# Reordering the front part of an attention kernel: which engine normalizes, which maxima come first, and how many are done when the loop begins

## The chip, the cores and the metric

The kernel runs on one core of a Trainium2 chip. The metric is the device time of one launch in microseconds (us), median over several runs. The engines are TensorE (PE, with PEld for its weight loads), VectorE (DVE), ScalarE (ACT), GpSimd (POOL) and SyncE (SP), which here issues nearly all transfers. Each engine takes its instructions strictly in the order in which the program lists them.

## The reference

One transformer layer on `x` of 2048 rows by 512 columns, in float32. It has 32 heads of 16 dimensions that share one key and one value head.

```
mod = silu(c) @ w_mod                      # six vectors: sa, ca, ga, sb, cb, gb
h = layernorm(x) * (1 + ca) + sa
q = h @ wq;  k = h @ wk;  v = h @ wv
o = softmax(q k^T / 4) v                   # for each of 32 heads
x = x + ga * (o @ wo)
h = layernorm(x) * (1 + cb) + sb
x = x + gb * (gelu(h @ w1 + b1) @ w2 + b2)
```

## The kernel before, in words

**Precision.** Products of full precision are made of three products of rounded operands: a tile is split into a high part (rounded) and a low part (the remainder), and high x high, low x high and high x low are added in one bank (`mm3`, line 162). A "set" below is such a group of three.

**Units and the loop.** The attention is cut into 64 units: eight blocks of 256 query rows, and in each block eight groups of four heads. The order of work is written out by hand: the program is recorded in the order in which Python issues it, and each engine keeps that order. A unit needs first the maximum of each row of scores, found by *max products*: a matmul of queries and 512 keys into one of three PSUM buffers named m (line 505), and a reduction on DVE (line 510). There are 32 for each unit, half of them on the upper 64 rows of the PE array and half on the lower 64, where pairs run side by side. When a unit's 32 are done, `put_max` reduces them once more (558), transposes (559), arranges the result (`gather`, 553), splits it into a high part mh and a low part ml, and sends these as extra rows into the unit's query tile `qst` (548): the score product of the exponentials (line 607) then comes out with the maximum subtracted, and ACT takes the exponentials (611). Products with the values (628) add to the unit's output.

The loop goes over units, in pairs of steps, four pairs for each unit. A pair holds eight score products and eight exponentials for its unit, and some max products for later units; beside these it holds pieces of query projections (line 191), whose result DVE copies out (456). How far the max products run ahead is set by `lead`: `lead[0]` is 32 + 4 x `LEAD_0` (56 done when the loop begins), and for the first eight units it rises evenly to 312 at the ninth; in a pair, the number issued is rounded to an even number.

**The front part.** Before the loop, x is loaded in four blocks of 512 rows, and for each block b:

- `stats1`: mean and variance on DVE (199 to 205), inverse root on POOL (207), and the factors for ACT (354, 355);
- `xhat1`: the normalized rows, four row tiles, on DVE, ACT (364) or POOL (366);
- `heads`: for each quarter of the columns, transposes (`turn1`, 373), modulation on ACT (`mod1`, 379), rounding (132 on ACT or 130 on POOL) and remainder (137);
- `keys`: four sets against the joined key and value weights (162), then `kv_out`: two casts of the keys into `ks` (394) and a copy to `vt` (395), both on ACT;
- `low_k`: the low part of the keys on DVE, written to rows 32 to 48 of `ks` (400); `repeat_k`: ACT copies it to rows 96 to 112 (404), for the lower half of the array;
- `v_out`: transposes of the values (412) and a copy (413).

Once block b's keys stand in `ks`, max products with 512 more keys can be made. So the front runs max products of the first two units between the other steps. `FIRST_MAX` gives their order as pairs of unit and block of keys; `SLOTS` gives the order of everything else: each entry is a number of max products, and then the named steps. "q 1" is a query projection, "rows" the late modulation rows (290), "wq" a weight's preparation. `keep_warm` issues filler matmuls (285). At the end of the front come the first score products (607, at 74.85 us in the trace).

## Time and profile before

| what | value |
|---|---|
| median of 3 runs | 1565.62 us (1565.11 to 1568.13) |
| span of the profiled execution, first to last instruction | 1563.1 us |
| the profiled execution's own time | not listed apart from its span |
| granted TensorE clock, mean | 1.000 |
| PE busy | 1546.5 us (99%) |
| DVE busy | 1401.7 us (90%) |
| ACT busy | 1228.8 us (79%) |
| POOL busy | 681.7 us (44%) |
| first score product of the loop | 74.85 us |

The times in the trace count from the span's start. A busy share is an average over stages: the front part (to about 75 us), the loop over 64 units, and the end. A row of the timeline gives the start, the length, the engine, the line of the kernel, the operation, the tile written and the tiles read, and how many instructions were merged into the row (x4); in brackets stands the idle time before it, and who ended it.

### The profile page before, as it was taken

To read this page: it belongs to the slowest core of one execution; us is meant where nothing else is said; L and a number is where in the kernel's file an instruction comes from. 1 tells how busy PE (TensorE), PEld (TensorE's weight loads), DVE (VectorE), ACT (ScalarE), POOL (GpSimd) and SP (SyncE) were. 2 spreads that over 40 slices of the span, in tenths; PEclk is the share of its full clock that TensorE was granted. 3 is DMA by queue.
4 is the path that set the end of the run, shared out by engine and by line. 5 is a ranking of instruction groups with operands and counts; after the bars stand their busy time and mean duration, and the time that the engine had idled before them with its cause. 6 is when DMAs were issued, how large, how long until landed. Compare 5 with 4: busy or idle time off the path is not lost.

```text
span 1563.1 us, 41433 instructions
## 1 busy us (share of the span) xinstructions
PE 1546.5 (99%) x16387; PEld 959.9 (61%) x16387; DVE 1401.7 (90%) x2479; ACT 1228.8 (79%) x2392; POOL 681.7 (44%) x1194
## 2 busy tenths in 40 slices
PE   7999999999999999999999999999999999999999
PEld 4455555567655665557655675556655676556667
DVE  7999999999999999999999999999999999999625
ACT  5577778788777887788877887788877888788853
POOL 5545433877323570246422472245611573235711
PEclk9999999999999999999999999999999999999999
DMA  7235412313030211213022120303112130312241
GB/s 244 97 96 194 152 52 89 120 52 97 19 110 19 83 60 35 93 29 99 29 62 69 57 84 26 105 16 97 43 50 79 46 97 20 102 34 66 81 150 61
DMA packets 83126, 121.63 MB, mean 78 GB/s; under 512 B 19614, under 2 KB 56222, under 8 KB 82676
## 3 DMA queue, kind: packets, MB, share of 16 engines
q1 hardware_dynamic: 82916, 118.97, 23.5%
q8 instruction: 130, 2.13, 0.6%
q14 instruction: 64, 0.52, 0.1%
q10 hardware_dynamic: 16, 0.00, 0.0%
HBM read 91.13 MB, written 27.27 MB: 76 GB/s over the span
## 4 chain that ended last, share of the span: by engine, by line
PE 84%; DVE 10%; issue 3%; POOL 2%; DMA 1%; ACT 0%; ACTq 0%; SPq 0%; POOLq 0%; DVEq 0%
PE acc L628 28%; PE m L505 24%; PE e L607 16%; DVE mx L510 8%; PE w1ps L191 8%; PE w2ps L181 2%; PE w2ps L191 1%; PE w1ps L181 1%; DMA xt<-in_A_x_dram 1%; PE qps L191 1%; PE tp L191 1%; PE wops L191 1%; PE kps L162 1%; DVE st L835 1%; DVE x L828 1%
## 5 line engine op out<-in xcount | busy, mean ns | idle before, releaser
L510 DVE TENSOR_REDUCE mx<-m 128x1 f32<-128x512 f32 x2048 | 1270.5, 682 | 86.9 <-PE m L505 63.8
L611 ACT ACTIVATE p<-e 128x512 f32<-128x512 f32 x2048 | 1099.3, 598 | 257.4 <-PE e L607 110.5
L505 PE MATMUL m<-ks,qst 64*128 64x512 f32 x2048 | 832.4, 429 | 1.9 <-DVE mx L510 0.6
L607 PE MATMUL e<-qst,ks 64*128 64x512 f32 x2048 | 747.6, 412 | 0.1
L628 PE MATMUL acc<-p,va 128*32 128x256 f32 x8192 | 548.0, 385 | 0.0
L505 PEld LDWEIGHTS m<-ks,qst 64*128 64x128 f32 x2048 | 366.5, 184 | 212.3 <-DVE mx L510 174.8
L607 PEld LDWEIGHTS e<-qst,ks 64*128 64x128 f32 x2048 | 362.5, 184 | 95.2 <-ACT p L611 71.1
L628 PEld LDWEIGHTS acc<-p,va 128*32 128x32 f32 x8192 | 213.7, 109 | 213.1 <-issue 110.0
L553 POOL TENSOR_SCALAR mt<-turned 8x32 f32<-8x32 f32 x256 | 53.1, 208 | 418.9 <-DVE turned L559 406.9
L191 PE MATMUL w1ps<-h2H,w1t 64*128 64x256 f32 x1232 | 235.6, 287 | 0.0
L191 PEld LDWEIGHTS w1ps<-h2H,w1t 64*128 64x128 f32 x1232 | 185.8, 184 | 28.9 <-DVE mx L510 17.7
L191 PE MATMUL w1ps<-h2L,w1t 64*128 64x256 f32 x616 | 169.2, 275 | 0.0
L191 PE MATMUL w2ps<-w2H,gH 64*128 64x512 f32 x284 | 123.8, 436 | 0.0
L191 PEld LDWEIGHTS w1ps<-h2L,w1t 64*128 64x128 f32 x616 | 114.0, 185 | 0.0
L191 PE MATMUL w2ps<-w2L,gH 64*128 64x512 f32 x282 | 110.9, 393 | 0.0
L191 PE MATMUL w2ps<-w2H,gL 64*128 64x512 f32 x282 | 110.2, 391 | 0.0
L954 POOL TENSOR_SCALAR tt<-tt 128x256 f32<-128x256 f32 x77 | 31.0, 403 | 142.6 <-ACT tt L953 109.3
L137 POOL TENSOR_TENSOR gL<-z,gH 128x256 fp32r<-128x256 f32 x77 | 57.0, 740 | 6.4
L955 POOL TENSOR_TENSOR tt<-tt,z 128x256 f32<-128x256 f32 x77 | 56.7, 736 | 6.4
L965 POOL TENSOR_TENSOR z<-tt,z 128x256 f32<-128x256 f32 x77 | 56.4, 733 | 6.0
L964 POOL TENSOR_TENSOR tt<-tt,z 128x256 f32<-128x256 f32 x77 | 56.4, 732 | 0.0
L191 PEld LDWEIGHTS w2ps<-w2H,gL 64*128 64x128 f32 x282 | 52.2, 185 | 0.4
(190 smaller groups left out, 1480.9 us busy)
## 6 DMA issues: line engine op xcount, KB each, us to landing
w1t<-dw SPq DMA_DIRECT2D x82, 512.0 KB
qst<-dq SPq DMA_DIRECT2D x384, 32.0 KB
do<-oc SPq DMA_DIRECT2D x64, 128.0 KB
dw<-w1s SPq DMA_DIRECT2D x11, 512.0 KB
xt<-in_A_x_dram SPq DMA_DIRECT2D x4, 1024.0 KB
dq<-qH SPq DMA_DIRECT2D x16, 256.0 KB
dq<-qL SPq DMA_DIRECT2D x16, 256.0 KB
x<-in_A_x_dram SPq DMA_DIRECT2D x8, 512.0 KB
```

The source lines that it names most:

```text
L137: eng_l.tensor_tensor(out=dst_l, in0=src, in1=raw(dst_h), op=ALU.subtract)
L181: nc.tensor.matmul(ps, a, b_, start=first_, stop=last_)
L191: ins = nc.tensor.matmul(ps, a[rows], b_[rows], start=first_ and s == 0, stop=last_ and s == 1)
L505: nc.tensor.matmul(m, qsts[u][rows, j, t * P:(t + 1) * P], ks[rows, kc * 512:(kc + 1) * 512], start=True, stop=True)
L510: nc.vector.tensor_reduce(out=self.mx[u][:, i, kc:kc + 1], in_=m, axis=AX.X, op=ALU.max)
L553: nc.gpsimd.tensor_scalar(out=mt[:, g:g + 32], in0=turned[g:g + 4 * T, :], scalar1=1.0, scalar2=0.0, op0=ALU.mult, op1=ALU.add)
L607: nc.tensor.matmul(e, ks[rows, kt * P:(kt + 1) * P], rhs, start=True, stop=True)
L611: ins = nc.scalar.activation(dst, e, AF.Exp, scale=0.25)
L628: ins = nc.tensor.matmul(accs[u][32 * cidx:32 * cidx + 32, :], va[:, kt, :], rhs, start=kt == 0, stop=kt == NKT - 1)
L955: nc.gpsimd.tensor_tensor(out=tt, in0=tt, in1=z, op=ALU.mult)
L964: nc.gpsimd.tensor_tensor(out=tt, in0=tt, in1=z, op=ALU.mult)
L965: nc.gpsimd.tensor_tensor(out=z, in0=tt, in1=z, op=ALU.add)
```

## The change

Eight edits, all for the front part and the first units:

- Of block 3's four normalized row tiles, POOL makes two and ACT the last two ("xhat 3" in `SLOTS`).
- The low part of the keys of blocks 0 and 3 is made by DVE for both row groups (`both`), and ACT's copy of it is dropped for these two blocks.
- The last remainder of block 3 goes from POOL to DVE.
- Block 1's normalization is split one and three around the first query projection, not two and two; block 3's statistics are no longer interleaved with block 1's heads.
- `FIRST_MAX` has a count for each part: the first unit's maxima come ahead of more of the second's, and end at the 42nd max product, not the 48th.
- The first unit's maxima are arranged and split by DVE; for the first eight units the last reduction comes at once, and the sends two ticks earlier.
- `SLOTS` has another order: heads and keys interleaved, 48 max products in all; `LEAD_0` is 4, so the loop begins with 48 done. The loop makes up for the other eight in its first eight units, 33 for each instead of 32.
- 10 filler matmuls instead of 16, and two more fillers dropped.

```diff
-LEAD_0 = 6
-FIRST_MAX = ((0, 0), (1, 0), (0, 1), (1, 1), (0, 2), (0, 3), (1, 2), (1, 3))
-SLOTS = ((2, "keys 1", "keys 1"), (2, "keys 1", "keys 1"), (2, "low 1", "heads 2"), (2, "heads 2", "k 1"), (1, "warm"), (1, "heads 2"), (2, "heads 2", "v 0"),
-         (2, "heads 3"), (2, "heads 3"), (2, "heads 3"), (2, "heads 3"), (0, "keys 2"), (2, "keys 2"), (2, "keys 2"), (2, "keys 2"),
-         (2, "low 2", "k 2", "v 1", "wq 1"), (0, "keys 3"), (2, "keys 3"), (2, "keys 3"), (2, "keys 3"), (2, "low 3", "k 3"),
-         (0, "v 2"), (2, "q 1"), (2, "q 1"), (2, "q 1"),
-         (2, "q 1", "rows"), (2, "v 3", "wq 2"), (2, "rows"), (2, "rows"), (2, "rows", "wq 3", "load"))
+LEAD_0 = 4
+FIRST_MAX = ((0, 0, 4), (1, 0, 1), (0, 1, 4), (1, 0, 3), (0, 2, 4), (1, 1, 1), (0, 3, 4), (1, 1, 3), (1, 2, 4), (1, 3, 4))
+SLOTS = ((0, "keys 1"), (2, "keys 1", "keys 1", "keys 1"), (2, "heads 2"), (2, "heads 2"), (2, "low 1", "k 1", "heads 2"),
+         (2, "heads 2", "xhat 3"), (2, "v 0"), (2, "keys 2"), (2, "keys 2", "heads 3"), (2, "keys 2", "heads 3"),
+         (2, "keys 2", "v 1"), (2, "heads 3", "low 2", "k 2"), (2, "heads 3", "keys 3"), (2, "wq 1", "v 2"), (2, "keys 3"),
+         (2, "keys 3", "keys 3"), (0, "low 3"), (2, "q 1"), (2, "q 1", "v 3"), (2, "q 1"), (2, "q 1", "wq 2"),
+         (2, "rows"), (2, "rows"), (2, "rows"), (2, "rows", "wq 3", "load"))
-WARM = (4, 16, 2, 5)
+WARM = (4, 10, 2, 5)
...
-    def xhat1(b, eng):
+    def xhat1(b, eng, late=0):
...
-            if eng is nc.scalar:
+            if eng is nc.scalar or t >= QT - late:
...
-    def low_k(b):
+    def low_k(b, both=False):
         cols = slice(b * BQ, (b + 1) * BQ)
-        nc.vector.tensor_tensor(out=ks[32:48, cols], in0=kps.pop(b)[32:48, :], in1=raw(ks[32:48, cols]), op=ALU.subtract)
+        ps = kps.pop(b)
+        for r in (32, 96) if both else (32,):
+            nc.vector.tensor_tensor(out=ks[r:r + 16, cols], in0=ps[r:r + 16, :], in1=raw(ks[r:r + 16, cols]), op=ALU.subtract)
...
-            begin = [o for u, kc in FIRST_MAX for o in products(u, [kc])]
+            parts = {(u, kc): products(u, [kc]) for u in range(2) for kc in range(NKC)}
+            begin = [parts[u, kc].pop(0) for u, kc, n in FIRST_MAX for _ in range(n)]
...
         def gather():
+            eng = nc.vector if u == 0 else nc.gpsimd
             for g in range(0, P, 32):
-                nc.gpsimd.tensor_scalar(out=mt[:, g:g + 32], in0=turned[g:g + 4 * T, :], scalar1=1.0, scalar2=0.0,
-                                        op0=ALU.mult, op1=ALU.add)
-            split(mh, ml, mt, nc.gpsimd, nc.gpsimd)
+                eng.tensor_scalar(out=mt[:, g:g + 32], in0=turned[g:g + 4 * T, :], scalar1=1.0, scalar2=0.0,
+                                  op0=ALU.mult, op1=ALU.add)
+            split(mh, ml, mt, eng, eng)
...
-            later(MAX_WAIT[1], send)
-        if NQ <= u < NQ + 2:
+            later(MAX_WAIT[1] - (2 if u < NQ else 0), send)
+        if u < NQ + 2:
             reduce()
...
-            mod1(b, d, pool if d == 1 else act, dve if b == 1 and d > 1 else pool)
+            mod1(b, d, pool if d == 1 else act, dve if b == 1 and d > 1 or (b, d) == (3, KD - 1) else pool)
...
-    run(rows, 2)
+    run(rows, 1)
...
-    low_k(0)
+    low_k(0, True)
...
-    def last_h(t):
-        if t == QT - 1:
-            run(h1)
-    stats1(3, last_h)
+    stats1(3)
+    run(h1)
     load_mods(2)
-    repeat_k(0)
     run(xhat1(2, act))
-    run(xhat1(3, pool))
+    rows3 = xhat1(3, pool, 2)
+    run(rows3, 2)
     keep_warm(WARM[1])
```

More of the change, by code (lines that the diff above doesn't have):

```diff
@@ L1288, in adaln_mqa_mlp @@
             "v 0": one(v_out, 0), "v 1": one(v_out, 1), "v 2": one(v_out, 2), "v 3": one(v_out, 3), "rows": late_rows(),
-            "low 1": one(low_k, 1), "low 2": one(low_k, 2), "low 3": one(low_k, 3), "k 1": one(repeat_k, 1), "k 2": one(repeat_k, 2), "k 3": one(repeat_k, 3), "load": one(load_q, 2), "warm": warm(),
+            "low 1": one(low_k, 1), "low 2": one(low_k, 2), "low 3": one(low_k, 3, True), "k 1": one(repeat_k, 1), "k 2": one(repeat_k, 2), "xhat 3": one(run, rows3), "load": one(load_q, 2), "warm": warm(),
             "wq 1": one(prep_wq, 1), "wq 2": one(prep_wq, 2), "wq 3": one(prep_wq, 3)}
```

## The prediction

> **What bounds the kernel now.** I read the page first, then busy time by stretch, then the timeline of the front part, then the chain of waits.

> ```profile
> span 1563.1 us, 41433 instructions
> PE 84%; DVE 10%; issue 3%; POOL 2%; DMA 1%; ACT 0%; ACTq 0%; SPq 0%; POOLq 0%; DVEq 0%
> 33.00:75.60 42.60, 41.91 (x194) 21.51 (x195) 37.58 (x61) 23.46 (x43) 28.28 (x32) 1.00 0.32 117
> 98.00:121.00 23.00, 23.00 (x246) 13.62 (x242) 21.30 (x38) 17.89 (x35) 12.56 (x18) 1.00 0.49 159
> ```

> The chain that ended last runs 84% over PE and 10% over DVE: these two are to be followed. The two stretches give busy time of PE, PEld, DVE, ACT and POOL, then the granted clock. In the front (33.0 to 75.6) DVE is busy 37.58 of 42.60 us: 5.0 us of waits at most can be won on it. In the loop it is busy 21.30 of 23.00. So a max product (matmul on PE, reduction on DVE) moved from front to loop leaves an engine with little room and enters another with little room. The sum has two terms: when the first exponentials' product starts (74.85 now, the loop's start), and what eight more max products cost in the first eight units.

> **Front, before.** Each row is start, length, engine, line, operation.

> ```profile
> 30.07 0.69 DVE L137 TENSOR_TENSOR bigL<-h,bigH 128x512 fp32r<-128x512 f32 x1 [0.27 <-ACT bigH L132]
> 31.40 0.62 ACT L404 CAST ks<-ks 16x512 fp32r<-16x512 f32 x1
> 32.04 2.93 ACT L364 ACTIVATE xt<-xt,nm,rs 128x512 f32<-128x512 f32 x4
> 32.99 1.29 DVE L510 TENSOR_REDUCE mx<-m 128x1 f32<-128x512 f32 x2
> 34.43 0.49 PE L505 MATMUL m<-ks,qst 64*128 64x512 f32 x2
> 34.96 1.29 DVE L510 TENSOR_REDUCE mx<-m 128x1 f32<-128x512 f32 x2 [0.68 <-PE m L505]
> 36.55 1.17 ACT L394 CAST ks<-kps 48x512 fp32r<-48x512 f32 x2 [1.58 <-PE kps L162]
> 37.73 0.58 ACT L395 COPY vt<-kps 32x512 f32<-32x512 f32 x1
> 38.34 0.68 DVE L400 TENSOR_TENSOR ks<-kps,ks 16x512 fp32r<-16x512 f32 x1
> 41.11 0.78 ACT L379 ACTIVATE h<-tp,sa,ca 128x512 f32<-128x512 f32 x1
> 42.45 0.77 ACT L379 ACTIVATE h<-tp,sa,ca 128x512 f32<-128x512 f32 x1
> 42.80 0.66 PE L373 MATMUL tp<-ident,xt 128*128 128x128 f32 x4
> 49.45 0.62 ACT L132 CAST bigH<-h 128x512 fp32r<-128x512 f32 x1
> 51.83 1.19 ACT L394 CAST ks<-kps 48x512 fp32r<-48x512 f32 x2 [1.75 <-PE kps L162]
> 57.86 1.18 ACT L394 CAST ks<-kps 48x512 fp32r<-48x512 f32 x2 [1.90 <-PE kps L162]
> 66.63 2.48 DVE L510 TENSOR_REDUCE mx<-m 128x1 f32<-128x512 f32 x4 [1.03 <-PE m L505]
> ```

> and lengths on PE from the chain of waits:

> ```profile
> 28.10 3.64 PE idle L285 x16
> 34.93 1.59 PE kps L162 x6
> 45.33 0.59 PE tp L373 x4
> 50.47 0.42 PE m L505
> 50.89 0.90 PE kps L162 x3
> 65.17 0.99 PE modl L290 x8
> ```

> From them: a reduction 0.62 (2.48 for 4); a pair of max products 0.42 on PE, ready for DVE 0.53 after its start; a set of three key or query products 0.90, or 0.70 behind another set; four transposes 0.59; one reduction's idle filler 0.23; a modulation group 0.99; a normalized row tile on ACT 0.73; modulate plus round 1.34 (42.45 less 41.11). The low part of the keys starts after the copy to vt (38.34 against 38.31). A pair with a set costs PE 1.32, DVE 1.24: PE paces slightly.

> **Front, after, in the order in which the changed program's instructions stand.** I put each step behind its engine's previous step and its inputs.

> 1. *Block 0.* DVE makes both low parts (2 x 0.68), so ACT's copy at L404 goes and its normalization of block 2 starts at 31.40 and ends at 34.35. Ten fillers instead of 16 free PE 6 x 0.23 = 1.4 us early. Block 1's four sets with one pair between, and the second half of qst that the pair needs (estimated 0.65 us earlier, since its query copy stands behind one row tile fewer), end at 34.5. Its casts begin there, not at 36.55: 2.0 us won. DVE is free for its first maximum at about 32.5, an estimate from 32.99: the extra low part falls into waits like the 0.27 at 30.07.
> 2. *ACT.* Casts and vt 1.79, modulate plus round 1.34, modulate 0.78: 38.4. The copy of low 1 comes next in order and waits for DVE, which starts the third max at 35.0, does six and low 1 (with 0.2 of waits) until 39.4. Copy 0.62: 40.1; two modulate plus round: 42.8; then the two row tiles of block 3 taken from GpSimd, 2 x 0.73: 44.2. Block 3's first transposes need them; now they run at 42.80. So 1.4 us later, and DVE runs dry for 0.6.
> 3. *PE* from 44.2: pair, set, transposes, pair, set (0.42 + 0.90 + 0.59 + 0.42 + 0.90, with 0.4 of switches): block 2's keys are done at 47.8, casts now at 51.83. 4.0 us won. DVE waits 1.2 in three holes, as PE paces.
> 4. *Given back.* Behind these casts ACT has casts and vt 1.79, a value copy 0.2, modulate plus round 1.34, a copy 0.64, modulate plus round 1.40: block 3's last rounding ends at 53.3; now it ends at 49.45 + 0.62 = 50.07. Its remainder is DVE's now, queued ahead of the max products with block 2's keys. DVE has its 24 maxima and low 2 done at 51.9, waits 1.4, subtracts (0.69, as at 30.07) and goes on at 54.0. Behind it wait 18 reductions of this unit, and PE, whose three m buffers are full from 53.2 to 54.6.
> 5. Set, two pairs, sets 3 and 4 (0.90 + 0.70): block 3's keys at 58.0, casts now at 57.86. The whole lead is gone. Casts and vt 1.79, then two low parts instead of one: 61.2. DVE is dry from 57.8 to 59.85.
> 6. Twelve maxima of the first unit are left: two pairs at DVE's 1.24, four at PE's 1.32 to 1.42, 0.2 of switches: last one at 69.4, where now it is 66.63 + 2.48 = 69.11. Six products fewer stand ahead of it (42 against 48), and the waits of steps 4 and 5 take them up.

> **From the last maximum to the loop.**

> ```profile
> 69.15 0.19 DVE L558 TENSOR_REDUCE mm<-mx 128x8 f32<-128x32 f32 x1
> 69.37 0.21 DVE L559 STREAM_TRANSPOSE turned<-mm 128x32 f32<-128x32 f32 x1
> 69.67 1.02 POOL L553 TENSOR_SCALAR mt<-turned 8x32 f32<-8x32 f32 x4 [0.33 <-DVE turned L559]
> 70.78 0.29 POOL L130 TENSOR_SCALAR mh<-mt 8x128 fp32r<-8x128 f32 x1
> 71.09 1.44 ACTq L548 DMA_DIRECT2D qst<-mh  x1
> 74.85 0.25 PEld L607 LDWEIGHTS e<-qst,ks 64*128 64x128 f32 x2 [0.51 <-DMA qst<-ml]
> 9.88 0.17 DVE L205 TENSOR_SCALAR ve<-mv 128x4 f32<-128x4 f32 x1
> 9.49 0.36 DVE L203 BATCH_NORM_AGGREGATE mv<-st 128x2 f32<-128x6 f32 x4
> ```

> GpSimd has mh ready 1.96 after the last maximum (71.07 less 69.11). On DVE the trace shows no such piece: four small operations lie between 0.36 (last row) and 4 x 0.17, mh about 0.18; with reduction and transpose 1.07 to 1.39; I take 1.2. From mh to the product e it is 3.78 (two issues on ACT's queue, the transfer); nothing in that changes. e: 69.4 + 1.2 + 3.78 = 74.4, so **0.5 us earlier**. The six maxima and five fillers between (DVE free 69.4 + 1.6 + 6 x 0.62 = 74.7) hide under the transfer; were it gone, they would cost that much.

> Bounds of this term: no wait on DVE at all from its first maximum (step 1, 32.5) gives 32.5 + 42 x 0.62 + 5 x 0.69 = 62.0, e at 67.0, 7.9 us earlier; each hole a little longer (vt, switches) 1 us later.

> **Loop.** 264 max products instead of 256 in the first eight units: by the rounding in the code, ten instead of eight in the first pair of steps of the second, fourth, sixth and eighth unit, five in each of its two steps.

> ```profile
> 97.36 2.48 DVE L510 TENSOR_REDUCE mx<-m 128x1 f32<-128x512 f32 x4 [0.36 <-PE qps L191]
> 98.67 1.07 PE L628 MATMUL acc<-p,va 128*32 128x256 f32 x16
> 101.51 1.07 PE L628 MATMUL acc<-p,va 128*32 128x256 f32 x16
> 101.40 0.68 DVE L456 COPY q<-qps 128x512 f32<-128x512 f32 x1
> 224.89 2.49 DVE L510 TENSOR_REDUCE mx<-m 128x1 f32<-128x512 f32 x4 [0.23 <-PE e L607]
> 92.07 0.23 PE e L607
> ```

> A step is 2.84 (101.51 less 98.67); DVE idles 0.36 in it. PE's two row halves are evenly filled, so a fifth product lengthens one by 0.23: 8 x 0.23 = 1.8 us is the low end. The high end is 8 x 0.62 = 5.0. The copy of a projection (0.68 on DVE, 101.40) falls into three of the four pairs, where the room is used up: demand 10 x 0.62 + 0.68 = 6.9 against 5.68 + 0.46 = 6.14, a lag of 0.76, of which three m buffers hide about 0.35; 0.46 + 0.4 = 0.9 each. The fourth pair (0.23 of idle a step, no copy) 0.6. Sum **3.3 us**. The first units' sends stand two ticks earlier in SP's queue, behind GpSimd's gather: queued behind them are loads of query tiles and weight pieces, the former two pairs (11.4 us) ahead of their use; I cost it at nothing, one step (2.8) if that cover were gone. From the ninth unit on the order is the same.

> **Sum.** -0.5 + 3.3 = +2.8. The profiled execution spans 1563.1 and has no time of its own beside it; the median, 1565.62, lies 2.5 above and I carry that: 1568.4. About 0.2% (3.1 us) is what a measurement can tell from no change: 1562.5 to 1568.75. The forecast lies just inside.

> **Rivals.** *The front's holes close (faster).* If keys of blocks 2 and 3 come as early as step 3 says and steps 4 and 5 cost nothing, 3.5 us go, and with the loop's low end: 1565.62 - 4.0 + 1.8 = 1563.4; with all waits gone 1565.62 - 7.9 + 3.3 = 1561.0. For it: 5.0 us of DVE waits stand there to be won; against: DVE and ACT take their work in the order given.
> *The loop pays in full (slower).* DVE becomes the loop's pace: +5.0 - 0.5: 1570.1. It decides where DVE's lag at the end of a pair exceeds what three m buffers hold (0.35 by my count). For it: 21.30 of 23.00; against: the idle 0.36 a step.
> *The clock drops (slower).* My front holds PE 2.1 us at 59.8; the row of 33.00:75.60 shows 1.00, its holds included. Were the clock halved over two pairs, 2 x 1.33 is added: 1568.4 + 2.7 = 1571.1. [...]
> *It doesn't do what it says:* the first unit's maxima end no earlier. That is my step 6.

> **Numbers.** Forecast 0.55, its spread (1 us either way in the front, 0.8 in the loop) lying half above 1568.75; holes close 0.25, half of it beyond 1562.5; full price 0.15; clock 0.05. Faster 0.14; slower 0.22 + 0.15 + 0.05 = 0.42; same 0.44. The range, 1562.5 to 1571.2, leaves out the best front and the worst of clock and loop; the forecast's own is 1566.6 to 1570.

> **What would show it.** Casts of blocks 1, 2, 3 at 34.5, 47.8, 58.0; DVE waiting for block 3's last rounding at 52 and for vt at 59; first e near 74.4; pairs with ten products 0.6 to 0.9 longer. Wrong would be an e before 71, or those pairs unlengthened.

## The result, and the profile after

The changed kernel takes 1576.47 us (median of 4 runs, 1575.8 to 1579.15), the kernel before 1565.36 beside it (1564.17 to 1568.13). The ratio is 1.0075, with a 95% interval of 1.0061 to 1.009: slower by 11.1 us. The forecast was 1568.4, its range ended at 1571.2.

The page of the kernel after, its span and the shares of the chain that ended last:

```profile
span 1574.0 us, 41409 instructions
PE 85%; DVE 11%; DMA 1%; POOL 1%; ACT 1%; issue 0%; SPq 0%; DVEq 0%
```

The shares hardly differ from those before, and PE is busy for 99% in both: the page doesn't show where 11 us went. Busy time by stretch does. The columns are the stretch, its length, busy time of PE, PEld, DVE, ACT and POOL with instructions in brackets, the granted clock, the DMA share and GB/s. Kernel after:

```profile
38.91:42.32 3.41, 3.09 (x14) 1.56 (x13) 3.38 (x6) 3.32 (x6) 3.20 (x4) 1.00 1.04 431
42.32:45.73 3.41, 3.41 (x12) 2.25 (x11) 1.45 (x3) 2.02 (x5) 1.06 (x1) 0.50 0.99 411
52.56:55.97 3.41, 1.91 (x9) 1.04 (x9) 2.17 (x4) 1.91 (x5) 2.06 (x3) 1.00 0.00 0
55.97:59.38 3.41, 3.41 (x9) 1.99 (x8) 2.21 (x4) 0.00 (x0) 0.00 (x0) 0.50 0.00 0
62.80:66.21 3.41, 2.17 (x11) 1.23 (x11) 2.95 (x5) 0.21 (x1) 0.00 (x0) 1.00 0.02 5
66.21:69.62 3.41, 3.41 (x10) 1.88 (x8) 2.37 (x4) 0.00 (x0) 0.00 (x0) 0.50 0.00 0
73.04:76.45 3.41, 2.11 (x16) 0.62 (x18) 3.20 (x12) 0.00 (x0) 1.08 (x3) 1.00 0.21 80
76.45:79.86 3.41, 3.41 (x12) 1.19 (x13) 2.06 (x5) 0.73 (x2) 1.65 (x3) 0.50 0.15 32
```

Read them in pairs. Four times the granted clock falls to 0.50 for 3.41 us (a cut, below). In the 3.41 us ahead of three of these cuts PE is busy for only 1.91 to 2.17 us; ahead of the first for 3.09. In the halved stretches PE is busy throughout and looks fully used, but the products of a key set start 0.43 us apart there (42.90 and 43.33) and 0.23 ahead of the cut (41.32 and 41.55). DVE, busy for 37.58 of 42.60 us in the front before, has 1.45 to 2.37 of 3.41 there. The kernel before has 1.00 from 33 to 75.6.

The timeline of the kernel after, at the places that the prediction named:

```profile
48.34 1.17 ACT L394 CAST ks<-kps 48x512 fp32r<-48x512 f32 x2 [0.49 <-PE kps L162]
53.80 0.69 DVE L137 TENSOR_TENSOR bigL<-h,bigH 128x512 fp32r<-128x512 f32 x1 [1.35 <-ACT bigH L132]
60.08 1.18 ACT L394 CAST ks<-kps 48x512 fp32r<-48x512 f32 x2 [5.58 <-PE kps L162]
73.14 0.19 DVE L562 TENSOR_REDUCE mm<-mx 128x8 f32<-128x32 f32 x1
75.03 1.43 ACTq L551 DMA_DIRECT2D qst<-mh  x1
80.69 0.50 PE L611 MATMUL e<-qst,ks 64*128 64x512 f32 x2
84.43 1.07 PE L632 MATMUL acc<-p,va 128*32 128x256 f32 x16
269.41 1.07 PE L632 MATMUL acc<-p,va 128*32 128x256 f32 x16
```

and the last two places in the kernel before:

```profile
78.59 1.07 PE L628 MATMUL acc<-p,va 128*32 128x256 f32 x16
258.61 1.07 PE L628 MATMUL acc<-p,va 128*32 128x256 f32 x16
```

The first score product e starts 5.84 later (80.69 against 74.85), and so does the first product with the values (84.43 against 78.59). At the ninth unit the distance is 10.80 (269.41 against 258.61), and it stays between 10.7 and 11.1 to the end. So the front (up to the start of the loop) lost 5.84 us and the first eight units 4.96; the other 56 units lost nothing. These two numbers are what the experiments have to explain.

### The profile page after: what moved, and what is told of

Its sections match the earlier page's. It is cut to its first block, busy times and chain, and to the rows that moved or that the text cites. A ratio compares the mean times of both kernels' runs of the same rounds, so it can differ in the third digit from the quotient of the medians.

```text
span 1574.0 us, 41409 instructions
## 1 busy us (share of the span) xinstructions
PE 1552.0 (99%) x16379; PEld 963.0 (61%) x16379; DVE 1404.7 (89%) x2488; ACT 1229.5 (78%) x2392; POOL 675.7 (43%) x1185
## 4 chain that ended last, share of the span: by engine, by line
PE 85%; DVE 11%; DMA 1%; POOL 1%; ACT 1%; issue 0%; SPq 0%; DVEq 0%
PE acc L632 29%; PE m L508 24%; PE e L611 15%; DVE mx L513 9%; PE w1ps L191 8%; PE w2ps L191 2%; PE w2ps L181 2%; PE qps L191 1%; PE w1ps L181 1%; DMA xt<-in_A_x_dram 1%; PE tp L191 1%; PE kps L162 1%; DVE st L839 1%; PE wops L191 1%; DVE x L832 1%; PE wops L181 0%
## 5 line engine op out<-in xcount | busy, mean ns | idle before, releaser
L191 PE MATMUL w1ps<-h2H,w1t 64*128 64x256 f32 x1232 | 235.1, 287 | 0.0
L191 PEld LDWEIGHTS w1ps<-h2H,w1t 64*128 64x128 f32 x1232 | 185.6, 184 | 28.9 <-DVE mx L513 19.8
L191 PE MATMUL w1ps<-h2L,w1t 64*128 64x256 f32 x616 | 169.0, 274 | 0.0
L191 PE MATMUL w2ps<-w2H,gH 64*128 64x512 f32 x284 | 124.2, 437 | 0.0
L191 PEld LDWEIGHTS w1ps<-h2L,w1t 64*128 64x128 f32 x616 | 113.7, 185 | 0.0
L191 PE MATMUL w2ps<-w2L,gH 64*128 64x512 f32 x282 | 110.9, 393 | 0.0
L191 PE MATMUL w2ps<-w2H,gL 64*128 64x512 f32 x282 | 110.3, 391 | 0.0
L137 POOL TENSOR_TENSOR gL<-z,gH 128x256 fp32r<-128x256 f32 x77 | 57.1, 742 | 6.4
L959 POOL TENSOR_TENSOR tt<-tt,z 128x256 f32<-128x256 f32 x77 | 56.9, 739 | 6.4
L191 PEld LDWEIGHTS w2ps<-w2H,gL 64*128 64x128 f32 x282 | 52.3, 185 | 1.1
```

What stands on the lines that cost most here:

```text
L137: eng_l.tensor_tensor(out=dst_l, in0=src, in1=raw(dst_h), op=ALU.subtract)
L191: ins = nc.tensor.matmul(ps, a[rows], b_[rows], start=first_ and s == 0, stop=last_ and s == 1)
L959: nc.gpsimd.tensor_tensor(out=tt, in0=tt, in1=z, op=ALU.mult)
```

## The experiments

I read every run by the same two numbers: how much later than in the kernel before (78.59 and 258.61) the first product with the values starts, and how much of the distance is added by the ninth unit. A filler is a matmul whose result nobody reads. The edits of c1_lead0 and of e5_pool to e9_rows are shown against e1_fill, those of the runs b and r against the kernel before; each run's full edit can be longer than the cut shown (...).

### The front: the clock

**e1_fill.** The changed kernel, with 25 fillers in four places where PE waits. The theory was that the clock is cut because PE has too little to do in a window.

```
-    (2, "heads 2", "xhat 3"), (2, "v 0"), ...
+    (2, "heads 2", "xhat 3"), (1, "warm x"), (1, "v 0"), ...        # 3 fillers
...
+    "warm v": 7 fillers ahead of block 3's second set; "warm e": 9 ahead of "v 3";
+    "warm f": 6 ahead of the last modulation rows
```

> The changed kernel with 25 filler matmuls (128 rows, 512 columns) put where PE holds in the front: 3 before the max product that waits for block 1's repeated low keys, 7 and 9 before the two that wait for a free m buffer, 6 before the last pair. Theory A (the clock was cut in four stretches of 3.4 us, each behind a stretch with little PE work): clock 1.000, first score product near 74.8 instead of 80.69, time 1576.5 - 5.9 = 1570.6. Theory B (the waits of DVE and ACT alone delay the loop): first score product at 80 to 80.7, time 1576, whatever the clock.

Measured: 1570.79 us, ratio 1.0042 (1.0027 to 1.0057); the clock is 1.000. Rows of its timeline:

```profile
47.66 1.17 ACT L394 CAST ks<-kps 48x512 fp32r<-48x512 f32 x2 [0.49 <-PE kps L162]
53.12 0.69 DVE L137 TENSOR_TENSOR bigL<-h,bigH 128x512 fp32r<-128x512 f32 x1 [1.34 <-ACT bigH L132]
58.16 1.17 ACT L394 CAST ks<-kps 48x512 fp32r<-48x512 f32 x2 [4.34 <-PE kps L162]
59.95 1.39 DVE L402 TENSOR_TENSOR ks<-kps,ks 16x512 fp32r<-16x512 f32 x2 [2.10 <-ACT vt L395]
69.74 0.19 DVE L562 TENSOR_REDUCE mm<-mx 128x8 f32<-128x32 f32 x1
71.62 1.43 ACTq L551 DMA_DIRECT2D qst<-mh  x1
74.59 1.43 PE L285 MATMUL idle<-wkH 128*128 128x512 f32 x5
75.95 0.50 PE L611 MATMUL e<-qst,ks 64*128 64x512 f32 x2
```

25 fillers make the kernel 5.7 us faster. The product e starts at 75.95: of the 5.84 us, 1.10 remain. The loop adds 4.98, as without fillers. Part of the 1.10 is only the run's start. Block 0's casts stand ahead of everything that was reordered, and move by tenths from run to run; in the kernel before and in e1_fill:

```profile
24.84 1.16 ACT L394 CAST ks<-kps 48x512 fp32r<-48x512 f32 x2
25.39 1.16 ACT L394 CAST ks<-kps 48x512 fp32r<-48x512 f32 x2
```

From these casts to e it is 50.02 us before, 55.90 after (the casts at 24.79) and 50.56 here; the other five runs with this front and these fillers, or with one edit to it (e5_pool), have 50.52 to 50.58. So the four cuts cost 5.3 us, and 0.5 remain. The kernel before is itself no surer than some tenths: r1_now, with nearly its front, has 49.50.

**e2_half.** The same 25 fillers, on 64 rows of the array. The edit reached further than meant: it also halved the rows of the ten fillers that stand ahead of `SLOTS` and of the five ahead of e.

```
-            nc.tensor.matmul(ps, wkH[:, 0, :], wkH..., start=True, stop=True)
+            rows_ = slice(0, 64) if mods_late else slice(0, P)
+            nc.tensor.matmul(ps, wkH[rows_, 0, :], wkH[rows_]..., start=True, stop=True)
```

> As the kernel with 25 fillers, but each filler on 64 rows of the array only: the same number, the same length. If the gate counts idle time, it is as that kernel: clock 1.000, first score product near 74.8, about 1570.6. If it counts work by rows, the stretches behind the second to fourth hold stay below the mark (estimated 40 to 46% of full rows, from the stretches that were followed by a cut and those that were not): two or three cuts remain, first score product at 78 to 80, 1574 to 1576.

Measured: 1576.02 us in one run, all of the gain of e1_fill gone. Two cuts of 6.83 us, at 29.13 and 56.44. Ahead of the first only the ten fillers (28.02 to 31.10) differ, so that not all of the loss is the 25 fillers'. Ahead of the second and in it:

```profile
53.03:56.44 3.41, 3.13 (x15) 1.93 (x14) 2.03 (x4) 3.30 (x8) 1.46 (x2) 1.00 0.00 0
56.44:63.26 6.82, 6.82 (x18) 3.98 (x17) 3.82 (x7) 0.18 (x3) 1.43 (x2) 0.50 0.01 2
```

PE was busy for 3.13 of 3.41 us ahead of this cut, with 15 matmuls. The kernel after has a window with less of both, which no cut followed:

```profile
59.39:62.80 3.41, 2.40 (x9) 1.04 (x7) 0.91 (x2) 1.74 (x3) 0.00 (x0) 1.00 0.00 0
```

So neither busy time nor the number of matmuls decides it alone.

**e9_rows.** The clean form of it: the 25 fillers on 64 rows, the other fifteen untouched.

```
-        keep_warm(n, **place())
+        keep_warm(n, rows=64, **place())
```

> The kernel of the change with the same 25 fillers in the same places, on 64 rows of the array and not on 128; the other fillers are untouched. Theory (the clock is judged by PE's time weighted by the rows in use, in windows of 3.4 us, with a mark between 1.37 and 1.58 us of full rows): the four windows ahead of the cuts had 1.32, 0.52, 1.04 and 1.37, and get about 0.35, 0.8, 1.0 and 0.7 more, so that the second alone (1.3) stays below the mark: one cut near 56, none at 42, 66 and 76; time about 1572.1 (one cut, 1.3 us more than with full rows). Rival (PE's busy time or idle gaps decide, whatever the rows): no cut, 1570.8. Second rival (matmuls on half the rows do not count at all): cuts as without fillers, about 1576.

Measured: 1570.57 us in one run, no cut. The forecast of one cut missed. I had added the fillers to the windows of the kernel after, but by my placing they lie elsewhere in this run, which has no cut in the front to mark them: they begin at 49.66 and 53.07, and the hole, which lay in one window at 52.56, is shared by two. The first of them:

```profile
49.66:53.07 3.41, 3.12 (x15) 1.94 (x14) 2.04 (x4) 3.30 (x8) 1.46 (x2) 1.00 0.00 0
```

From the casts of block 0 to e it is 49.96 us, 0.6 less than with full-height fillers and no more than before (50.02). So the 0.5 that remained in e1_fill may be only what its full-height fillers cost PE; this is one run.

To see what the clock follows, I summed for each window of 3.41 us the streaming time of PE's matmuls times the share of the array's 128 rows in use, over all 18 kernels of this study. The window is taken from the cuts: they last 3.41 or 6.83 us, and in the kernel after they begin at 42.32, 55.97, 66.21 and 76.45, which is 4, 3 and 3 times 3.41 apart. Streaming time is counted back from the end of each record, and is an estimate: 0.21 us for 512 columns at a clock of 1.00, half of the 0.43 between starts at 0.50 (42.90 and 43.33 in the kernel after), and twice that per column where the operands are not rounded (of the products with the values, four side by side, twelve take 0.85 us and sixteen 1.07, so 0.22 for 256 columns more); matmuls on 32 columns each that run side by side share one count. The windows ahead of the four cuts in the kernel after have 1.25, 0.46, 0.97 and 1.24 us. All 15 cuts in the fronts follow a window of 0.45 to 1.32. From 24 to 90 us the lowest windows without a cut have 1.32 (e9_rows), 1.34 (e3_lead4) and 1.36 (r3_64); the lowest in the kernel before has 1.56. So by these sums, an estimate from these 18 traces alone, the mark lies near 1.3 of 3.41 us. The sum is no finer than about 0.1: counted from the starts of the records, two windows without a cut (1.18 and 1.23) lie among those with one. Without the weight the two kinds overlap more: 2.04 us of streaming was followed by a cut (e2_half, 53.03), 1.78 was not (r3_64, 59.32).

The window at 49.66 in e9_rows, shown above, and the one at 53.03 in e2_half hold the same 15 matmuls at the same places within 0.01 us, and both have 1.32. One was followed by a cut and the other was not. So these two sit on the mark, e9_rows had some luck, and what decides there is not shown.

**e5_pool.** Step 4 of the prediction, in e1_fill: block 3's last remainder goes back to GpSimd.

```
-  dve if b == 1 and d > 1 or (b, d) == (3, KD - 1) else pool
+  dve if b == 1 and d > 1 else pool
```

> The kernel of the change with the 25 fillers that keep the clock up (the run e1_fill), and block 3's last remainder on GpSimd again. Tests step 4 of the prediction by itself. Theory (DVE's wait of 1.34 us for that rounding, and the subtraction of 0.69 behind it, hold up reductions and products): GpSimd has the remainder at 54.4, 0.6 later than DVE, and DVE is 2.0 us ahead; block 3's casts start near 56.9 and not at 58.16, the exponentials' product 1 to 1.3 earlier than 75.95, time about 1569.6. Rival (PE and block 3's keys pace, the wait lies in slack): casts and product within 0.4 of 58.16 and 75.95, time 1570.8.

Measured: 1570.85 us, ratio 1.0038 (1.0024 to 1.0051). Block 3's casts are at 57.73 (0.43 earlier), e is at 75.51 (0.44 earlier), and the time is that of e1_fill. Rows of its timeline:

```profile
47.24 1.17 ACT L394 CAST ks<-kps 48x512 fp32r<-48x512 f32 x2 [0.48 <-PE kps L162]
52.47 1.87 PE L285 MATMUL idle<-wkH 128*128 128x512 f32 x7
54.80 0.69 DVE L513 TENSOR_REDUCE mx<-m 128x1 f32<-128x512 f32 x1 [1.54 <-PE m L508]
```

Block 2's casts, ahead of the edit, are 0.42 earlier too (47.24 against 47.66): the run began earlier, and the edit gained nothing. The rival holds, but the run can't say why. Seven fillers of e1_fill stand in PE's queue at this place, and the product behind them starts 1.80 after the first of them in both runs (54.27 and 54.71). DVE no longer waits 1.34 for the rounding, and waits 1.54 for PE instead. What the wait costs without fillers was not measured.

**b1_order, b2_holes, b3_tail.** The front's main idea alone, on the kernel before: the first unit complete after 44 max products.

```
-FIRST_MAX = ((0, 0), (1, 0), (0, 1), (1, 1), (0, 2), (0, 3), (1, 2), (1, 3))
+FIRST_MAX = ((0, 0, 4), (1, 0, 4), (0, 1, 4), (1, 1, 2), (0, 2, 4), (0, 3, 4), (1, 1, 2), (1, 2, 4), (1, 3, 4))
```

> The kernel before with one part of the change alone: the first unit's maxima ahead, counted out product by product, so that the first unit is complete after 44 max products and not after 48. Slots, engines, the arranging on GpSimd and the 56 products ahead of the loop stay as they were. Theory (what the order alone is worth where the bricks around it stay): four reductions of 0.62 fewer ahead of the first unit's last maximum, which ends near 66.6 and not at 69.1; four more stand behind it, ahead of the first exponentials' product, so that this starts near 73.0 and not at 74.85. No gate cut. Time 1.9 us below the kernel before, about 1563. Rival (block 3's keys set the end of the first unit's maxima, not the count ahead of them): the last maximum ends within 0.5 of 69.1, and the time is that of the kernel before.

Measured: 1571.75 us, ratio 1.0048 (1.0034 to 1.0062): 7 us slower where 1.9 faster was expected. By stretch:

```profile
54.12:57.53 3.41, 2.42 (x8) 1.21 (x9) 2.10 (x5) 1.62 (x5) 1.61 (x3) 1.00 0.00 0
57.53:60.94 3.41, 3.41 (x8) 1.67 (x8) 2.51 (x4) 0.00 (x0) 0.32 (x2) 0.50 0.00 0
60.94:64.36 3.42, 1.49 (x9) 0.70 (x8) 2.10 (x4) 2.39 (x5) 0.00 (x0) 1.00 0.02 5
64.36:71.18 6.82, 6.82 (x14) 3.33 (x14) 3.83 (x6) 0.17 (x1) 0.00 (x0) 0.50 0.00 0
```

In the order before, four products of the second unit stand between block 1's and block 2's products. Without them PE reaches a product with block 2's keys at 54.08, which are ready at 54.90: it holds 0.88 us, with the rest of its queue behind it. One hole of that size and the waits that follow leave 1.07 us of work in the window (by the sum above), the clock halves, block 3's keys come late, PE holds again, and the clock halves for two windows more.

b2_holes closes these two holes with useful work: two of block 3's sets ahead of the first product with block 2's keys, two query sets and three fillers ahead of the first with block 3's.

```
-  (0, "keys 3"), (2, "keys 3"), (2, "keys 3"), (2, "keys 3"), (2, "low 3", "k 3"), (0, "v 2"), (2, "q 1"), (2, "q 1"), (2, "q 1"), (2, "q 1", "rows"), ...
+  (0, "keys 3", "keys 3"), (2, "keys 3"), (2, "keys 3"), (2, "low 3", "k 3"), (0, "v 2", "q 1"), (2, "q 1"), (0, "q 1", "warm b"), (2, "q 1"), (2, "rows"), ...
```

> The order of the run b1_order (first unit complete after 44 products) with the holes closed in which PE stood still and after which the clock was cut: two of block 3's key sets next to each other ahead of the first product with block 2's keys, query projections next to each other ahead of the first product with block 3's, and three fillers. Theory (the order is worth 1.9 us, as forecast for b1_order, once the clock stays up): the first unit's last maximum near 67, the first exponentials' product near 73, no cut, time about 1563.4. Rival (block 3's keys and PE's order set the last maximum, not the count): last maximum within 0.5 of 69.1, time within 0.6 of the kernel before; if a cut comes, 1.3 us each on top.

Measured: 1567.93 us, ratio 1.0018 (1.0009 to 1.0027). Both cuts are gone; another stands at 74.97. DVE:

```profile
63.48 5.23 DVE L511 TENSOR_REDUCE mx<-m 128x1 f32<-128x512 f32 x8 [1.04 <-PE m L506]
68.75 0.19 DVE L559 TENSOR_REDUCE mm<-mx 128x8 f32<-128x32 f32 x1
69.11 7.54 DVE L511 TENSOR_REDUCE mx<-m 128x1 f32<-128x512 f32 x12
```

The first unit's last maximum is at 68.71; the kernel before and the three runs with its order (r1_now, r3_64, r2_48) have 69.11, 68.97, 69.72 and 69.97. Counted from block 0's casts it is 43.3 us against 44.0 to 44.8, so the order is worth 0.6 to 1.5 us there, not 2.5. Behind it now stand twelve maxima, 7.54 us, where the kernel before has eight: PE is held by its m buffers, does little in that window (0.71 us by the sum above), and is cut.

b3_tail puts one filler behind each of the last eight products.

```
     while mp.done < lead[0]:
         chunk(1)
+        keep_warm(1, **ebank())
```

> The run b2_holes with one filler behind each of the eight max products between the slots and the loop, where its clock was cut at 75.0 after a window with only 0.7 us of full rows. Theory (the order is worth what b2_holes showed at the first unit's last maximum, 68.74 where runs of the kernel before have 69.1 to 70.0, and the cut alone hid it): no cut, the exponentials' product near 74.2, time 0.5 to 1.2 below the kernel before, about 1563.8. Rival (the twelve maxima behind the first unit's last set the product, not the arranging and the sends): product at 75 or later, time 1564.6 to 1566.

Measured: 1570.08 us, ratio 1.0037 (1.0024 to 1.0049), with a spread of 1567.6 to 1573.2 over six runs: the rival, and worse. A full-height filler between two products on 64 rows costs PE 0.43 us and not 0.23, the products come 0.86 apart, and the window at 72.51 still has only 1.26 us; the cut comes at 75.92. Whether the order alone gains with the clock up was therefore not shown. What was shown is that it moves the first unit's last maximum (here to 67.53, 42.7 us behind block 0's casts) by 0.6 to 2.1 us, and then pays in the queue behind it.

### The loop: the price of eight max products

**c1_lead0.** The changed kernel with fillers, and 56 products ahead of the loop.

```
-LEAD_0 = 4
+LEAD_0 = 6
```

> The kernel of the change with the 25 fillers, and 56 max products ahead of the loop again and not 48, so that no pair of the first units has ten. Theory: the loop's 5.0 us go, as the eight products are put where the first unit's arranging and sends are awaited; DVE has fourteen reductions instead of six behind the first unit's last maximum (near 69.7, arranging done near 71.5), the last products wait for the eleventh of them, so that the exponentials' product starts near 78.4 and not at 75.95: 1570.8 - 5.0 + 2.4 = 1568.2. Rival (the eight cost 0.62 each wherever they stand): product near 80.9, time 1570.8.

Measured: 1574.36 us, ratio 1.0059 (1.0045 to 1.0073). The first product with the values is 7.27 later than in the kernel before; a cut of 6.83 us at 76.31 is in it, so the front's part can't be read from this run. Its loop can: no pair has ten products, and it still loses 2.78 us, 0.44 to 0.46 in each of the first six units. That was new, and r1_now takes it up.

**r1_now.** The kernel before, with the last reduction at once in units 0 to 7.

```
-        if NQ <= u < NQ + 2:
+        if u < NQ + 2:
```

> The kernel before with one part of the change alone: the last reduction and the transpose of the maxima of units 0 to 7 at once and not at the next step. Theory (it costs its 0.4 us in each of units 1 to 7 wherever it is done at once): 1564.9 + 2.8 = 1567.7. Rival (its place matters only where pairs of ten have used up the room): 1564.9 within 0.5.

Measured: 1568.11 us, ratio 1.0017 (1.0008 to 1.0026). From the first product with the values to the ninth unit it loses 2.82 us, in steps of 0.42 to 0.50 a unit. DVE in the second unit:

```profile
101.48 0.68 DVE L456 COPY q<-qps 128x512 f32<-128x512 f32 x1
102.08 1.28 DVE L510 TENSOR_REDUCE mx<-m 128x1 f32<-128x512 f32 x2
103.39 0.19 DVE L558 TENSOR_REDUCE mm<-mx 128x8 f32<-128x32 f32 x1
103.68 0.21 DVE L559 STREAM_TRANSPOSE turned<-mm 128x32 f32<-128x32 f32 x1
```

Here the 0.40 us of reduction and transpose follow the projection's copy after two maxima; in the kernel before they stand at 105.59, six maxima behind the copy, and cost nothing. One edit of the change, harmless by its size, costs 2.8 us where the loop begins with 56 done.

**e7_late.** The same edit undone in the changed kernel with fillers, where the loop begins with 48.

```
-        if u < NQ + 2:
+        if u == 0 or NQ <= u < NQ + 2:
```

> The kernel of the change with the 25 fillers (the run e1_fill), and the last reduction and the transpose of the maxima of units 1 to 7 put off to the next step again, as the kernel before has it (unit 0's stay at once). The run with 56 products ahead had no pair of ten, and its loop still lost 0.4 us in each of the first seven units. Theory (the early reduction, 0.19 + 0.21 on DVE, falls between two maxima that PE's buffers wait for, and costs its length each time; the pairs of ten alone cost less than full price): the loop's cost falls from 5.0 to 2 to 3.3 us, time 1568 to 1569. Rival (the eight products pay 0.62 each, the early reduction lies in what they make idle): 1570.8 within 0.5.

Measured: 1570.95 us, ratio 1.0036 (1.0022 to 1.005); the loop costs 4.77, 0.2 less than in e1_fill. The rival: with 48 done a unit is complete eight products later, and the early reduction is nearly free. In e1_fill it stands at 110.04, ten maxima behind the copy at 102.97. The price of an edit hung on another edit.

**e8_send.** The early sends undone for units 1 to 7, in the changed kernel with fillers.

```
-            later(MAX_WAIT[1] - (2 if u < NQ else 0), send)
+            later(MAX_WAIT[1] - (2 if u == 0 else 0), send)
```

> The kernel of the change with the 25 fillers, and the sends of the maxima of units 1 to 7 two ticks later again, as the kernel before has them (unit 0's stays early; the reduction at once stays). Theory of the prediction (the early sends cost nothing, their issues lie in slack on SP's queue): 1570.8 within 0.4. Rival (the sends ahead of the loads of query tiles in SP's queue make PE wait, and are what costs 0.4 us a unit): the loop's cost falls by 2 to 2.8 us, time about 1568.4.

Measured: 1571.5 us, ratio 1.0039 (1.0025 to 1.0053), the loop 4.97. Early sends cost nothing, as forecast, and with the reduction early they gain nothing.

**r2_48.** The eight products alone: the kernel before, with 48 done when the loop begins and eight fillers in their place. Sends and reductions are as before.

```
-LEAD_0 = 6
+LEAD_0 = 4
-  (2, "rows"), (2, "rows"), (2, "rows", "wq 3", "load"))
+  (2, "rows"), (0, "rows", "warm a"), (0, "rows", "wq 3", "load", "warm b"))
```

> The kernel before with one part of the change alone: the loop begun with 48 max products done and not 56, and eight fillers on PE in the place of the eight (so that the clock is not cut there). Sends and reductions are as before. Theory of the prediction (slack in a step takes up part): the first exponentials' product, which waits for the sends, at 74.85 as before, the loop 2.0 to 3.3 longer: 1567 to 1568.7. Rival (eight times a reduction's 0.62, whatever is beside them): the loop 5.0 longer, 1570.4.

Measured: 1575.35 us, ratio 1.0066 (1.0053 to 1.0079). The first product e is at 74.94, as before (74.85): the eight products cost nothing in the front. Up to the middle of the fourth unit the loop loses 2.65 us, and e1_fill loses 2.64 there. So the eight products cost the loop this by themselves, whatever else was changed. What one step does is seen on PE, the fifth max product at its end (start, length, engine, line, operation):

```profile
101.70 0.42 PE L505 MATMUL m<-ks,qst 64*128 64x512 f32 x1
101.70 0.42 PE L607 MATMUL e<-qst,ks 64*128 64x512 f32 x1
102.09 0.49 PE L505 MATMUL m<-ks,qst 64*128 64x512 f32 x1
102.51 0.85 PE L628 MATMUL acc<-p,va 128*32 128x256 f32 x12
97.44 3.08 DVE L510 TENSOR_REDUCE mx<-m 128x1 f32<-128x512 f32 x5 [0.36 <-PE qps L191]
100.74 1.29 DVE L510 TENSOR_REDUCE mx<-m 128x1 f32<-128x512 f32 x2 [0.22 <-PE m L505]
```

A step has 4 max products, 4 score products and 6 of a projection, 14 matmuls on half the rows each, which run side by side in seven places 0.23 apart (the second 0.34 behind the first: 100.21, 100.55, and so on to 101.70). A fifth max product is the fifteenth: it stands alone in an eighth place, and starts 0.39 and not 0.23 behind the seventh, because it finds its three m buffers full until DVE ends a reduction at 102.03 (100.74 + 1.29). The step is 3.30 long and not 2.84: 0.46 for each of eight steps, 3.7 us, or 0.92 a pair. Behind it DVE lags, and the pairs that follow lose 0.1 to 0.4 each: 5.0 less 3.7, 1.3 us more in all.

Then, up to the start of the fifth unit, this run loses 3.96 us at one place, which the changed kernel doesn't:

```profile
168.95 0.57 SPq L548 DMA_DIRECT2D qst<-ml  x1
170.70 0.46 PE L607 MATMUL e<-qst,ks 64*128 64x512 f32 x1 [2.16 <-DMA qst<-ml]
```

The sends stand in SP's queue behind loads of query tiles, and come too late; PE waits 2.16, and the clock is cut at 171.1. This run has neither the early sends nor the early reduction. With either of them alone, in the changed kernel with fillers, the loop does not lose this: in e8_send (late sends, early reduction) the first of these sends is issued at 160.78, in e7_late (the reverse) at 161.92, both ahead of the loads, and here at 166.90, behind them.

**r3_64.** The other way: 64 done when the loop begins, so that four pairs have six.

```
-LEAD_0 = 6
+LEAD_0 = 8
```

> The kernel before with the loop begun with 64 max products done and not 56, so that four pairs of the first eight units have six and not eight. Theory (a product in the loop costs what it costs DVE): the front pays for eight reductions, less the 0.7 us in which DVE is dry ahead of the first exponentials' product, 4 to 5 us, and the loop gives 4 to 5 back: within 1 us of the kernel before, 1564.4 to 1566.4. Rival (with eight products a pair PE paces the loop, so six free only PE's 0.23 each): the front 4 to 5 longer, the loop 1.8 shorter, 1567.5 to 1568.5.

Measured: 1572.55 us, ratio 1.0059 (1.0042 to 1.0076). The front is 7.08 later, with a cut of 6.83 us at 76.38 in it; the loop gives nothing back up to there: the distance is 7.32 in the middle of the fourth unit (by the fifth it loses another 1.5, where e waits 1.29 for a send). Its steps with three max products:

```profile
103.19 1.07 PE L628 MATMUL acc<-p,va 128*32 128x256 f32 x16
106.03 1.07 PE L628 MATMUL acc<-p,va 128*32 128x256 f32 x16
108.87 1.07 PE L628 MATMUL acc<-p,va 128*32 128x256 f32 x16
```

2.84 again: thirteen matmuls need the same seven places as fourteen. So the price is a stair: from eight to six products a pair nothing, from eight to ten 0.92 and what lags behind.

**e6_odd.** The pairs of ten one pair later, where no copy stands beside them.

```
             goal = lead[u] + (lead[u + 1] - lead[u]) * (K + 2) / steps[u]
+            goal -= 0.3 if u < NQ else 0
```

> The kernel of the change with the 25 fillers, and the goal of the first eight units lowered by 0.3 of a product, which by the rounding puts the four pairs of ten max products one pair later, where DVE has no copy of a projection beside them. Theory of the prediction (slack of the step takes up part of it, the copies make the rest): 0.5 to 0.6 a pair, the loop's cost 2 to 2.5 us and not 5.0, time about 1568.2. Rival (full price: over a step DVE has no room that eight products could use, wherever they stand): 4 x 2 x 0.62 = 5.0 again, time 1570.8 within 0.5.

Measured: 1571.57 us, ratio 1.0041 (1.0028 to 1.0055), the loop 5.04: the rival. The units with a pair of ten, which has no copy beside it now, lose 1.03 to 1.48 each. The copy, on which the prediction built three of its four prices, was not what they cost.

**e3_lead4, e4_both.** Two attempts to let the eight products wait until the end: the loop never makes up for them.

```
-LEAD = 6
+LEAD = 4
```

in the changed kernel (e3_lead4), and the same in e1_fill with the early reduction and sends for all units (e4_both):

```
-            later(MAX_WAIT[1] - (2 if u < NQ else 0), send)
+            later(MAX_WAIT[1] - 2, send)
-        if u < NQ + 2:
+        if True:
```

> The changed kernel with LEAD 4 instead of 6 for all units: no pair of steps with ten max products, the eight products move to the last unit, in which no max product is left to run beside. Theory: the eight were paid in full by the loop (8 x 0.62 = 5.0): the loop's first eight units are as long as in the kernel before, first score product unchanged near 80.7, time 1576.5 - 5.0 = 1571.5. If they cost 3.3 as forecast: 1573.2. If maxima that are ready later hold the score products, or the last unit pays them: 1576 or more.

> Fillers and LEAD 4 together, and the last reduction and the sends early for all units. The two effects add: 1576.5 - 5.9 - 5.0 = 1565.6, no difference to the kernel before. If the front's waits are the cause and not the clock: 1571.

Measured: 1580.27 us, ratio 1.0103 (1.0086 to 1.012), and 1583.37 us, 1.0122 (1.0107 to 1.0137). In both the first eight units cost almost nothing (0.39 and 0.45): with no pair of ten, the 5 us are gone. They come back elsewhere. In e3_lead4 6.6 us are lost between units 9 and 13 (counted from 0), where sends are late again:

```profile
353.93 0.47 PE L611 MATMUL e<-qst,ks 64*128 64x512 f32 x1 [4.17 <-DMA qst<-ml]
```

with a clock cut at 354.31 behind it. In e4_both, which sends early everywhere, that wait is gone, but every unit loses 0.3 us from the ninth on, 17 in all; which of its two edits costs that was not separated.

No version that I ran beats the kernel before.

## Why the prediction was wrong

**The time** was 1576.47 for 1568.4. Of the 11.1 us, about 5.3 are the cuts and 0.5 the rest of the front (5.84 together; by e9_rows 5.9 and nothing), 5.0 are the loop, and 0.3 are not placed; the forecast had 0, -0.5 and +3.3.

**The failed step is the rival "the clock drops"**, held at 0.05 and priced at 2.7 us. I looked for one long wait of PE and found 2.1 us at 59.8; it came, 2.25 us at 61.8. That only a long wait would matter was my assumption. But the clock was cut four times, the first time after a window in which PE stood still for 0.32 us of 3.41, and the cuts cost 5.3 us. That work on PE holds the clock is shown by the fillers: with 25 of them its mean is 1.000 and not 0.996. That it counts by rows in use is the reading that fits the 18 traces best: a max product is on 64 of the 128 rows, and the front of max products with short waits came to 0.46 to 1.25 us in the four windows ahead of the cuts. I could have seen the risk in the profile before: the change takes six fillers and the two "warm" ones away and puts waits into steps 2 to 5, and the lowest window before already stood at 1.56 us by the sum above.

**The loop's term** was of the right kind and too small: 3.3 for 4.96. The rival "the loop pays in full" (0.15) had the number, 5.0, by luck (it is 3.7 and 1.3, not eight times 0.62), and half of the mechanism, the full m buffers. I let DVE's 0.36 us of idle time in a step count as room; it ends with a product of PE's (qps), and it stands in front of a group of five just as in front of four (97.44 in r2_48: five maxima, again 0.36). And I took PE's fifth product at 0.23 as the low end, without counting that fourteen matmuls fill seven places and a fifteenth, kept waiting for a buffer, costs 0.46. Early sends at nothing was right.

**The front's steps** held once the clock stayed up (e1_fill): casts of blocks 1, 2 and 3 at 34.67, 47.66 and 58.16 for 34.5, 47.8 and 58.0; DVE's wait for block 3's last rounding 1.34 for 1.4; low parts at 59.95 for 59.85; the last maximum at 69.71 for 69.4. That run began 0.55 later than the kernel before, so that these places are 0.2 to 0.7 earlier than forecast when counted from block 0's casts. In the kernel after, by contrast, with the clock cut, the casts of blocks 2 and 3 stand at 48.34 and 60.08 and the last maximum ends at 73.11. Two small terms missed. Arranging on DVE takes 1.83 (71.54 less 69.71), not 1.2: the four small operations take 1.09, as long as on GpSimd (1.02), where I had set them at 0.68 at most by a DVE row of another form. And from mh to e it is 4.4 for 3.78: the five fillers ahead of e start only at 74.59, behind the last max products. I called these hidden, and they were late by 0.6. Together 1.2; less the 0.2 by which the last maximum came earlier than forecast, this is the 1.0 between -0.5 and +0.5.

**Step 4's price** stays open. DVE's wait was there at the time and of the size forecast, but to take it away gained nothing where seven fillers stood in PE's queue (e5_pool), and without them nobody took it away.

**"The front's holes close"** (0.25) did not come: block 3's keys were no earlier, as step 5 says.

## What to carry to other kernels

Before work is moved out of a stretch that is already short of matmuls, sum PE's streaming time by window, weighed by the rows in use, and not only its waits: here a window under about 1.3 of 3.41 us cost about 1.3 us each time (four cuts, 5.3 us). A price per moved operation was a stair here and not a slope (nothing from six to eight products a pair, 0.92 us from eight to ten, and what lags behind): count the places that a step has on PE, and whether the next operation needs one more. And an edit's cost is read with the other edits in place: the early reduction cost 2.8 us beside 56 products and 0.2 beside 48; and beside 48 the loop lost 4 us more at one place with neither the early reduction nor the early sends, and nothing there with either of them.
